# Sums of squares of the first four pairs taken by TensorE from the transposed rows, and an order of work planned with other durations

## The chip, the cores and the metric

The kernel runs on one core of one Trainium2 chip. The metric is the time of one execution on the device in microseconds. The median of three runs before the change is 1098.53 us (1098.04 to 1100.46).

## What is computed

A random-feature attention over 8 batches and 8 heads, followed by an MLP on its output.

```python
batch, n_heads, seq, head_dim = (8, 8, 576, 64)     # n_features m = 128
def phi(x):
    proj = np.einsum('bhsd,md->bhsm', x, omega)
    sq = np.sum(x * x, axis=-1, keepdims=True) / 2.0
    h = proj - sq
    h = h - np.max(h, axis=-1, keepdims=True)
    return np.exp(h) / np.sqrt(m)
q_p, k_p = (phi(q * scale), phi(k * scale))
kv = np.einsum('bhsm,bhsd->bhmd', k_p, v)
z = np.sum(k_p, axis=2)
num = np.einsum('bhsm,bhmd->bhsd', q_p, kv)
den = np.einsum('bhsm,bhm->bhs', q_p, z)[..., None] + 1e-06
attn = num / den
x = attn.transpose(0, 2, 1, 3).reshape(B * S, H * D)    # 4608 x 512
h = x @ w_in                                            # 512 x 2048
out = (h / (1.0 + np.exp(-h))) @ w_out                  # 2048 x 512
```

## The kernel before

Two heads make a pair: 32 pairs, n = 0 to 31, four to a batch. The 2 x 576 rows of a pair are nine blocks of 128 rows; the fifth (MID) holds the last 64 rows of the one head and the first 64 of the other. Each pair's queries and keys come in twice: `raw` (128 x 704, features on partitions, both heads above each other, and at the end a block of 128 columns for the mixed rows) and `nat` (128 x 9 x 64, rows on partitions).

For each pair and for k and q: `project` (L256) multiplies raw with omega on TensorE into two banks of PSUM, `project_mid` (L268) does the mixed block into a third; `square` (L248) squares nat in place on ACT, `square_sum` (L252) sums each row on DVE into `sq`; `top` (L272) takes the row maxima on DVE; `shift` (L280) makes the bias from maximum and sum of squares; `expo` (L294) takes the exponentials on ACT (from pair 8 on `lower` and `expo_all` do this in another way). Then `sums` (L314) adds the key features on POOL, `zsum` (L325) finishes that on TensorE and `zcopy` copies it; `kv`, `kt_copy`, `kv_turn` and `kw_copy` make the 128 x 64 matrices; `products`, `denom` (DVE) and `normal` (L372, POOL) normalise the queries; `turn` (L377) transposes them in three groups g = 0, 1, 2, `en_copy` copies these, and `numer` (L394) makes x, which `x_high` and `x_low` split into two float32r parts.

The MLP goes through nine column tiles of 512 tokens, t = 0 to 8, and in each through sixteen steps f of 128 hidden columns: `stage1` (s1, L489: for each k of the four pairs of a batch three matmuls), `silu` on ACT, `g_low` on DVE, and `stage2` (s2, L507) two steps later. So s1(0, f, k) needs x of pair k, and the first tile needs pairs 0 to 3. The weights arrive as 64-bit words; ACT (`exponent`), DVE (`word`, three operations) and POOL (`weight_high`, `weight_low`) make two float32r parts of each. w_out's are written to memory and read again for each tile.

The order of all this isn't written out. `Plan` (L64) holds units of work, each with an engine, an assumed duration, a key (a due time from `at` and `clock`), what it must follow (`after` for data, `order` for sequence alone) and the ring buffers and PSUM banks that it takes and frees. `Plan.run` simulates the engines and emits the units one by one; the framework then places the single instructions into each engine's queue, which runs in order, and may interleave those of neighbouring units. Pairs 0 to 3 (`LEAD = 4`, "calm" in the code) form the start, due every 11 us; the later pairs are due along the steps of the MLP. Pairs below 8 (`DIRECT`) take their exponentials from PSUM. nat has two buffers.

Of the kernel before, what the change touches and what calls it, by code (L numbers as in the profile page):

```python
# [197 lines left out]
def attention_mlp(ctx: ExitStack, tc: tile.TileContext, qT, kT, qn, kn, v, om_in, w_in, w_out, out):  # L198
# [10 lines left out]
    def new(tag, shape, dtype=F32):  # L209
        return ring.tile(shape, dtype, tag=tag, name=tag, bufs=RINGS[tag])  # L210
# [6 lines left out]
    oms = const.tile([P, M], F32, tag="oms", name="oms")  # L217
    prod = const.tile([P, NC, M + 1], F32, tag="prod", name="prod")
# [21 lines left out]
    def load_nat(n, who):  # L240
        T["nat", n, who] = nat = new("nat", [P, NC, D])
        nc.sync.dma_start(nat, (kn if who == "k" else qn)[divmod(n, NPAIR)])
# [5 lines left out]
    def square(n, who):  # L248
        nat = T["nat", n, who]
        nc.scalar.activation(nat, nat, AF.Square, scale=SCALE * 0.5**0.5)  # L250
# [17 lines left out]
    def project_mid(n, who, ps):  # L268
        nc.tensor.matmul(ps[:, :M], T.pop(("raw", n, who))[:, S:], oms, start=True, stop=True)  # L269
        T["p", n, who, 2] = ps  # L270
# [277 lines left out]
    for n in range(NWIN):  # L548
        calm = n < LEAD
        for i, who in enumerate("kq"):  # L550
# [3 lines left out]
            def prev(s):  # L554
                return [(s,) + x for x in last]
# [3 lines left out]
            before = [("nat", n, "k")] if i else ([("nat", n - 1, "q")] if n else [])  # L559
            add(("nat",) + w, "SP", 0.42, at(n, i - 13.5, 8.1 + 10 * i - 32), lambda n=n, who=who: load_nat(n, who),  # L560
                order=before, alloc=[("nat", ("nat",) + w)], lat=1.1)
            add(("sq",) + w, "ACT", 0.7, at(n, 2 * i - 4, 13 + 10 * i - 32), lambda n=n, who=who: square(n, who),
                after=[("nat",) + w])
            add(("ssum",) + w, "DVE", 0.78, at(n, 2 * i - 3, 14 + 10 * i - 32), lambda n=n, who=who: square_sum(n, who),
                after=[("sq",) + w], order=prev("ssum"), alloc=[(f"sq{who}", ("ss",) + w)], free=[("nat",) + w])
# [3 lines left out]
                after=[("raw",) + w, "omega"], order=prev("proj"),  # L569
# [3 lines left out]
            add(md, "PE", 0.25, at(n, 3 * i + 0.1, o + 5.2), lambda ps, n=n, who=who: project_mid(n, who, ps),  # L573
                banks=1, after=mid_after, free=[("raw",) + w])
# [5 lines left out]
            if calm:  # L580
                add(("nb", n, who, 0), "DVE", 0.45, at(n, 3 * i + 1.5, 0), lambda n=n, who=who: shift(n, who, every),
                    after=[("top", n, who, j) for j in range(3)] + [("ssum",) + w], free=[("ss",) + w])
            else:
                add(("nb", n, who, 0), "DVE", 0.5, at(n, 0, o + 1.4), lambda n=n, who=who: shift(n, who, sides),
                    after=[("top", n, who, j) for j in range(2)] + [("ssum",) + w])
                add(("nb", n, who, 2), "DVE", 0.4, at(n, 0, o + 5.8), lambda n=n, who=who: shift(n, who, middle),
                    after=[("top", n, who, 2), ("ssum",) + w], free=[("ss",) + w])
            for j in range(3):
                b = bk(md) if j == 2 else bk(pj, j)
                nb = ("nb", n, who, 0 if calm else j & 2)  # L590
                if n < DIRECT:
                    add(("exp", n, who, j), "ACT", 0.4 if j == 2 else 1.15,
                        at(n, 3 * i + 2 + 0.1 * j, o + 1.6 + (4.4 if j == 2 else 0.1 * j)),
                        lambda n=n, who=who, j=j: expo(n, who, j), after=[nb], table="exp", free=[b])
                else:
                    add(("low", n, who, j), "DVE", 0.36 if j == 2 else 0.7,
                        at(n, 0, o + 1.5 + (4.4 if j == 2 else 0.1 * j)),
                        lambda n=n, who=who, j=j: lower(n, who, j), after=[nb], free=[b])
# [9 lines left out]
        add(("sums", n), "POOL", 3.2, at(n, 6, 25), lambda n=n: sums(n), after=e["k"], order=[("sums", n - 1)] if n else [],  # L608
# [16 lines left out]
        add(("prod", n), "DVE", 1.7, at(n, 8, 34.2), lambda n=n: products(n),  # L625
# [4 lines left out]
        for g in range(3):  # L630
            add(("norm", n, g), "POOL", 0.85, at(n, 9 + 0.1 * g, 37 + 0.1 * g), lambda n=n, g=g: normal(n, g),
# [27 lines left out]
    def weight(i, key, src, last, more=()):  # L659
# [4 lines left out]
        for s in range(3):  # L664
            add(("wd",) + i + (s,), "DVE", (0.5, 0.78, 0.75)[s], key - 2 + 0.1 * s, lambda s=s: word(i, s),
                after=([("wd",) + i + (s - 1,), ("re",) + i] if s else [("wl",) + i]),
                order=[("wd",) + last + (0,)] if last and not s else [],
                alloc=[] if s else [("w32", ("w32",) + i)],
                free=([("wraw",) + i] if s == 2 else [("wre",) + i] if s == 1 else []))
        add(("wh",) + i, "POOL", 0.9, key - 1, lambda: weight_high(i), after=[("wd",) + i + (2,)], alloc=list(more))  # L670
        add(("wlo",) + i, "POOL", 1.05, key, lambda: weight_low(i), after=[("wh",) + i], free=[("w32",) + i])
# [102 lines left out]
```

## Time and profile before

| | us |
|---|---|
| median of three runs | 1098.53 |
| the profiled execution | 1101.4 |
| its span, first to last instruction | 1099.3 |
| TensorE busy in the span | 1053.1 |
| DVE, ACT, POOL busy | 566.4, 583.1, 255.5 |
| mean granted TensorE clock | 0.976 |

The profile is of one execution. A line of a group names the line of the kernel, the engine, the operation, the output and inputs by the program's names, their shape and the count, the busy time and the mean of one in ns, and then the time that the engine was idle just before and who ended that. A line of the timeline begins with its start and its length in us; neighbouring instructions of one kind are merged, and their count stands behind the x. A fp32 matmul appears as two records, its two passes. In the chain that ended last each row has start, length and what ran.

### The profile page before, as it was taken

To read this page: it belongs to the slowest core of one execution; us is meant where nothing else is said; L and a number is where in the kernel's file an instruction comes from. 1 tells how busy PE (TensorE), PEld (TensorE's weight loads), DVE (VectorE), ACT (ScalarE), POOL (GpSimd) and SP (SyncE) were. 2 spreads that over 40 slices of the span, in tenths; PEclk is the share of its full clock that TensorE was granted. 3 is DMA by queue.
4 is the path that set the end of the run, shared out by engine and by line. 5 is a ranking of instruction groups with operands and counts; after the bars stand their busy time and mean duration, and the time that the engine had idled before them with its cause. 6 is when DMAs were issued, how large, how long until landed. Compare 5 with 4: busy or idle time off the path is not lost.

```text
span 1099.3 us, 16192 instructions
## 1 busy us (share of the span) xinstructions
PE 1053.1 (96%) x5900; PEld 834.5 (76%) x5900; DVE 566.4 (52%) x1109; ACT 583.1 (53%) x1085; POOL 255.5 (23%) x327
## 2 busy tenths in 40 slices
PE   5677998899999999999999999999999999999998
PEld 4455776687877778777778777787877788888886
DVE  6788897745555455545555455555554431111111
ACT  5557878565556555555556555655565442222211
POOL 3666665411111111111111111111111110000000
PEclk7688999999999999999999999999999999999999
DMA  7576787553335443444345433533343226223323
GB/s 282 198 221 234 265 290 252 182 167 125 124 126 178 139 133 119 136 165 138 122 139 178 140 127 130 173 131 126 123 154 104 80 80 213 96 96 122 109 96 96
DMA packets 66526, 167.84 MB, mean 153 GB/s; under 512 B 15632, under 2 KB 15760, under 8 KB 66448
## 3 DMA queue, kind: packets, MB, share of 16 engines
q1 hardware_dynamic: 65984, 166.23, 45.6%
q8 instruction: 47, 0.77, 0.3%
q10 hardware_dynamic: 464, 0.59, 0.1%
q14 instruction: 31, 0.25, 0.1%
HBM read 146.87 MB, written 19.92 MB: 152 GB/s over the span
## 4 chain that ended last, share of the span: by engine, by line
PE 86%; DVE 5%; DMA 3%; ACT 3%; POOL 1%; issue 1%; SPq 0%; ACTq 0%; DVEq 0%; POOLq 0%
PE ps_acc L513 35%; PE ps_h L495 34%; PE ps_att L262 5%; PE ps_att L343 3%; PE ps_att L381 3%; PE ps_att L399 2%; DMA wraw<-w_out 1%; DMA nat<-qn 1%; PE ps_att L327 1%; PE ps_att L269 1%; DVE w L458 1%; ACT hq L298 1%; DVE w L462 1%; POOL hq L375 1%; DVE den L369 1%
## 5 line engine op out<-in xcount | busy, mean ns | idle before, releaser
L513 PE MATMUL ps_acc<-wo,gh 128*128 128x512 f32 x1152 | 369.9, 402 | 0.0
L500 ACT ACTIVATE gh<-ps_h 128x512 fp32r<-128x512 f32 x144 | 86.2, 599 | 295.9 <-PE ps_h L495 295.3
L505 DVE TENSOR_TENSOR gl<-ps_h,gh 128x512 fp32r<-128x512 f32 x144 | 99.1, 688 | 275.8 <-ACT ps_h L501 275.8
L513 PEld LDWEIGHTS ps_acc<-wo,gh 128*128 128x128 f32 x1152 | 207.1, 189 | 43.7
L495 PE MATMUL ps_h<-xh,wh 128*128 128x512 f32 x576 | 235.0, 409 | 0.3 <-ACT xh L413 0.3
L495 PE MATMUL ps_h<-xh,wl 128*128 128x512 f32 x576 | 226.7, 394 | 0.0
L495 PE MATMUL ps_h<-xl,wh 128*128 128x512 f32 x576 | 225.9, 392 | 0.0
L513 PE MATMUL ps_acc<-wo,gl 128*128 128x512 f32 x576 | 225.8, 392 | 0.0
L375 POOL TENSOR_TENSOR hq<-hq,rd 128x384 f32<-128x384 f32 x96 | 81.7, 879 | 421.4 <-DVE rd L370 396.5
L495 PEld LDWEIGHTS ps_h<-xh,wh 128*128 128x128 f32 x576 | 108.1, 188 | 24.7 <-issue 0.8
L513 PEld LDWEIGHTS ps_acc<-wo,gl 128*128 128x128 f32 x576 | 108.1, 188 | 24.2 <-issue 0.8
L495 PEld LDWEIGHTS ps_h<-xh,wl 128*128 128x128 f32 x576 | 108.1, 188 | 24.1
L495 PEld LDWEIGHTS ps_h<-xl,wh 128*128 128x128 f32 x576 | 108.5, 188 | 22.3 <-DVE xl L418 0.4
L312 ACT ACT_TABLE_LOAD x48 | 61.6, 1283 | 69.2 <-DVE hq L303 53.3
L318 POOL TENSOR_TENSOR t<-hk 128x256 f32<-128x256 f32 x64 | 48.8, 780 | 183.2 <-ACT hk L312 170.1
L278 DVE TENSOR_REDUCE mxq<-ps_att 128x4 f32<-128x512 f32 x57 | 37.2, 687 | 99.7 <-PE ps_att L262 99.6
L501 ACT ACTIVATE ps_h<-ps_h 128x512 f32<-128x512 f32 x144 | 85.3, 593 | 0.0
L500 ACT ACT_TABLE_LOAD x56 | 71.8, 1283 | 22.0 <-PE ps_h L495 21.3
L362 DVE TENSOR_TENSOR prod<-hq,zb 128x512 f32<-128x512 f32 (+1 forms) x96 | 52.3, 595 | 49.6 <-ACT zb L336 47.7
L250 ACT ACTIVATE nat<-nat 128x576 f32<-128x576 f32 x64 | 44.6, 703 | 20.3 <-DMA nat<-kn 12.3
L381 PE MATMUL ps_att<-ident,hq 128*128 128x128 f32 x261 | 41.1, 284 | 7.9 <-POOL wp L476 2.4
L278 DVE TENSOR_REDUCE mxk<-ps_att 128x4 f32<-128x512 f32 x55 | 35.6, 686 | 18.7 <-PE ps_att L262 18.7
(121 smaller groups left out, 1232.0 us busy)
## 6 DMA issues: line engine op xcount, KB each, us to landing
wo<-wo_d SPq DMA_DIRECT2D x144, 512.0 KB, 3.3
rawk<-kT SPq DMA_DIRECT2D x32, 352.0 KB, 3.0
rawq<-qT SPq DMA_DIRECT2D x32, 352.0 KB, 3.8
v<-v SPq DMA_DIRECT2D x32, 320.0 KB, 2.9
nat<-kn SPq DMA_DIRECT2D x32, 288.0 KB, 3.3
nat<-qn SPq DMA_DIRECT2D x32, 288.0 KB, 3.2
wraw<-w_in SPq DMA_DIRECT2D x16, 512.0 KB, 4.6
wraw<-w_out SPq DMA_DIRECT2D x16, 512.0 KB, 4.3
```

Of the source, the lines that this page charges most:

```text
L262: nc.tensor.matmul(ps[:, i * M : (i + 1) * M], raw[r, o : o + P], oms[r], start=True, stop=True)
L278: nc.vector.tensor_reduce(m[:, 5 * j : 5 * j + 4], ps.rearrange("p (c m) -> p c m", m=M), AX.X, ALU.max)
L312: nc.scalar.activation(h, h, AF.Exp)
L318: nc.gpsimd.tensor_tensor(t[:, j], e[:, 5 * j : 5 * j + 2], e[:, 5 * j + 2 : 5 * j + 4], ALU.add)
L362: nc.vector.tensor_tensor(prod[:, c, :M], e[:, c], zb[:, j].unsqueeze(1).broadcast_to([P, hi - lo, M]), ALU.mult)
L375: nc.gpsimd.tensor_tensor(e[:, c], e[:, c], rd[:, c].unsqueeze(2).broadcast_to([P, 3, M]), ALU.mult)
L381: nc.tensor.transpose(ps[:, i * P : (i + 1) * P], T["h", n, "q"][:, 3 * g + i], ident)
L495: nc.tensor.matmul(ph, w[:, k, :], x, start=k == 0 and n == 0, stop=k == NK - 1 and n == 2)
L500: nc.scalar.activation(gh, ph, AF.Silu)
L501: nc.scalar.activation(ph, ph, AF.Silu)
L505: nc.vector.tensor_tensor(gl, T["ph", t, f], T["gh", t, f].bitcast(F32), ALU.subtract)
L513: nc.tensor.matmul(T["po", t][j], g[:, js], w, start=f == 0 and n == 0, stop=f == NF - 1 and n == 2)
```

## The change

For pairs 0 to 3 nat is no longer loaded and DVE no longer sums rows. ACT squares the transposed rows (raw, 704 columns) into a buffer of the nat ring, now 704 columns wide. TensorE sums them over the 64 features of a head: nine matmuls with the squares as the stationary operand and one moving column, which has ones for the one head (`head`) or for both (the mixed block). They write nine columns beside the result of the middle block, and stand ahead of it; `shift` reads them from PSUM. So `mid` now waits for the squares, and a `proj` of these pairs is ordered behind the `mid` before it. From pair 4 on all is done as before. The plan also gets other durations for several units.

```diff
+    head = const.tile([P, 2], F32, tag="head", name="head")
+    nc.vector.memset(head, 0.0)
+    for j in range(2):
+        nc.vector.memset(head[j * D : (j + 1) * D, j : j + 1], 1.0)
...
     def load_nat(n, who):
-        T["nat", n, who] = nat = new("nat", [P, NC, D])
+        T["nat", n, who] = nat = new("nat", [P, S + P])[:, : NC * D].rearrange("p (c d) -> p c d", d=D)
...
     def square(n, who):
+        if n < LEAD:
+            T["rs", n, who] = rs = new("nat", [P, S + P])
+            nc.scalar.activation(rs, T["raw", n, who], AF.Square, scale=SCALE * 0.5**0.5)
+            return
...
     def project_mid(n, who, ps):
-        nc.tensor.matmul(ps[:, :M], T.pop(("raw", n, who))[:, S:], oms, start=True, stop=True)
+        raw = T.pop(("raw", n, who))
+        if n < LEAD:
+            rs = T.pop(("rs", n, who))
+            T["sq", n, who] = ps[:, M : M + NC]
+            for i in range(4):
+                for j in range(2):
+                    o = REST * j + i * P
+                    c = M + 5 * j + i
+                    nc.tensor.matmul(ps[:, c : c + 1], rs[:, o : o + P], head[:, j : j + 1], start=True, stop=True)
+            nc.tensor.matmul(ps[:, M + MID : M + MID + 1], rs[:, S:], ones[:, :1], start=True, stop=True)
+        nc.tensor.matmul(ps[:, :M], raw[:, S:], oms, start=True, stop=True)
...
+            if calm:
+                add(("sq",) + w, "ACT", 0.78, at(n, 3 * i - 0.5, 0), lambda n=n, who=who: square(n, who),
+                    after=[("raw",) + w], alloc=[("nat", ("nat",) + w)])
+            else:
...
             add(pj, "PE", 1.5, at(n, 3 * i, o), lambda a, b, n=n, who=who: project(n, who, a, b), banks=2,
-                after=[("raw",) + w, "omega"], order=prev("proj"),
+                after=[("raw",) + w, "omega"],
+                order=prev("proj") + ([("mid", n, "k")] if i else [("mid", n - 1, "q")] if n else []) * calm,
...
-            add(md, "PE", 0.25, at(n, 3 * i + 0.1, o + 5.2), lambda ps, n=n, who=who: project_mid(n, who, ps),
-                banks=1, after=mid_after, free=[("raw",) + w])
+            add(md, "PE", 1.6 if calm else 0.25, at(n, 3 * i + 0.1, o + 5.2), lambda ps, n=n, who=who: project_mid(n, who, ps),
+                banks=1, after=mid_after + ([("sq",) + w] if calm else []), free=[("raw",) + w] + ([("nat",) + w] if calm else []))
...
-        add(("sums", n), "POOL", 3.2, at(n, 6, 25), lambda n=n: sums(n), after=e["k"], order=[("sums", n - 1)] if n else [],
+        add(("sums", n), "POOL", 3.7 if n < DIRECT else 3.1, at(n, 6, 25), lambda n=n: sums(n), after=e["k"], order=[("sums", n - 1)] if n else [],
```

The other durations are `exp` 1.25 instead of 1.15, `prod` 2.1 instead of 1.7, `norm` 1.0 instead of 0.85, the three `word` operations 0.7, 0.85, 0.85 instead of 0.5, 0.78, 0.75, `wh` 0.8 instead of 0.9 and `wlo` 1.4 instead of 1.05.

What this does to the queues is seen in the program's order. POOL first, its first work of the attention. L318 to L323 before (L336 to L341 after) are a pair's key sums, L375 (L393) the normalisation of a pair's queries, L476 and L480 (L494 and L498) the two parts of a weight. Before:

```order
L318 TENSOR_TENSOR t<-hk 128x256 x2
L320 TENSOR_TENSOR es<-t 128x256
L323 TENSOR_TENSOR es<-es,hk 64x128 x2
L375 TENSOR_TENSOR hq<-hq,rd 128x384 x3
L476 CAST wh_322<-w_231 128x512
L318 TENSOR_TENSOR t<-hk 128x256
L480 TENSOR_TENSOR wl_323<-w_231,wh_322 128x512
L318 TENSOR_TENSOR t<-hk 128x256
L320 TENSOR_TENSOR es<-t 128x256
L323 TENSOR_TENSOR es<-es,hk 64x128 x2
```

The same place after:

```order
L336 TENSOR_TENSOR t<-hk 128x256 x2
L338 TENSOR_TENSOR es<-t 128x256
L341 TENSOR_TENSOR es<-es,hk 64x128 x2
L336 TENSOR_TENSOR t<-hk 128x256 x2
L338 TENSOR_TENSOR es<-t 128x256
L341 TENSOR_TENSOR es<-es,hk 64x128 x2
L393 TENSOR_TENSOR hq<-hq,rd 128x384 x3
L494 CAST wh_403<-w_260 128x512
L498 TENSOR_TENSOR wl_404<-w_260,wh_403 128x512
```

The sums of pair 1 stood behind the normalisation of pair 0 and interleaved with the first weight; now they stand ahead of both.

TensorE from the transposes of pair 0 to x of pair 0. hq is the queries of pair 0, es the key sums of pair 1, v is read by kv(1), en and kw by num(0), rawk is pair 2's. Before:

```order
L381 MATMUL ps_h_315<-ident_75,hq_156 128x128 x3
L381 MATMUL ps_att_329<-ident_75,hq_156 128x128 x3
L381 MATMUL ps_att_337<-ident_75,hq_156 128x128 x3
L327 MATMUL ps_h_412<-es_360,ones_80 128x256
L343 MATMUL ps_att_345<-hk_186,v_118 64x128 x10
L399 MATMUL ps_acc_370<-en_316,kw_266 64x512 x2
L399 MATMUL ps_att_371<-en_316,kw_266 64x64 x2
```

After, with the same names by role (L399 is the transposes now, L345 the key sums, L417 is num, L285 to L287 the group of the middle block with its squares):

```order
L399 MATMUL ps_acc_398<-ident_75,hq_166 128x128 x3
L399 MATMUL ps_acc_410<-ident_75,hq_166 128x128 x3
L399 MATMUL ps_acc_414<-ident_75,hq_166 128x128 x3
L345 MATMUL ps_acc_419<-es_325,ones_80 128x256
L285 MATMUL ps_acc_426<-head_84,nat_333 128x1 x8
L286 MATMUL ps_acc_426<-ones_80,nat_333 128x1
L287 MATMUL ps_acc_426<-oms_83,rawk_170 128x128
L417 MATMUL ps_h_450<-en_399,kw_292 64x512 x2
L417 MATMUL ps_h_451<-en_399,kw_292 64x64 x2
```

kv(1) has gone from between z(1) and num(0) to a place ahead of the transposes; the group of pair 2's keys has come in between.

ACT around the transposed queries of pair 2. en is their copy (L385 before, L403 after), hk the key exponentials of pairs 3 and 4, nat_604 and nat_739 are the queries of pair 4, nat_611 the keys of pair 5, hq_695 the queries of pair 3. Before:

```order
L442 ACTIVATE wre_639<-wraw_554 128x512
L250 ACTIVATE nat_604<-nat_604 128x576
L250 ACTIVATE nat_611<-nat_611 128x576
L385 COPY en_659<-ps_acc_658 128x384
L298 ACTIVATE hk_593<-ps_acc_583,nbk_595 128x128 x4
L298 ACTIVATE hk_593<-ps_att_584,nbk_595 128x128 x4
L385 COPY en_659<-ps_acc_680 128x384
```

After:

```order
L403 COPY en_773<-ps_acc_783 128x384
L403 COPY en_773<-ps_acc_788 128x384
L316 ACTIVATE hk_651<-ps_att_641,nbk_653 128x128 x4
L316 ACTIVATE hk_651<-ps_acc_642,nbk_653 128x128 x4
L258 ACTIVATE nat_739<-nat_739 128x576
L403 COPY en_773<-ps_att_772 128x384
L316 ACTIVATE hq_695<-ps_att_685,nbq_697 128x128 x4
L316 ACTIVATE hq_695<-ps_h_686,nbq_697 128x128 x4
```

The squares of pair 4's queries and pair 5's keys stood ahead of the first copy and of pair 3's key exponentials; now the first of them stands behind two copies and pair 4's key exponentials, and pair 3's query exponentials follow soon.

More of the change, by code (lines that the diff above doesn't have):

```diff
@@ L558, in attention_mlp @@
                 order=prev("raw"), alloc=[(f"raw{who}", ("raw",) + w)], lat=1.3)
[L559 to L565, printed above, removed]
+            if calm:
+                add(("sq",) + w, "ACT", 0.78, at(n, 3 * i - 0.5, 0), lambda n=n, who=who: square(n, who),
+                    after=[("raw",) + w], alloc=[("nat", ("nat",) + w)])
+            else:
+                before = [("nat", n, "k")] if i else ([("nat", n - 1, "q")] if n > LEAD else [("sq", n - 1, "q")])
+                add(("nat",) + w, "SP", 0.42, at(n, 0, 8.1 + 10 * i - 32), lambda n=n, who=who: load_nat(n, who),
+                    order=before, alloc=[("nat", ("nat",) + w)], lat=1.1)
+                add(("sq",) + w, "ACT", 0.7, at(n, 0, 13 + 10 * i - 32), lambda n=n, who=who: square(n, who),
+                    after=[("nat",) + w])
+                add(("ssum",) + w, "DVE", 0.78, at(n, 0, 14 + 10 * i - 32), lambda n=n, who=who: square_sum(n, who),
+                    after=[("sq",) + w], order=prev("ssum") if n > LEAD else [], alloc=[(f"sq{who}", ("ss",) + w)], free=[("nat",) + w])
             o = 6.2 + 10.8 * i
@@ L581, in attention_mlp @@
                 add(("nb", n, who, 0), "DVE", 0.45, at(n, 3 * i + 1.5, 0), lambda n=n, who=who: shift(n, who, every),
-                    after=[("top", n, who, j) for j in range(3)] + [("ssum",) + w], free=[("ss",) + w])
+                    after=[("top", n, who, j) for j in range(3)])
             else:
@@ L591, in attention_mlp @@
                 if n < DIRECT:
-                    add(("exp", n, who, j), "ACT", 0.4 if j == 2 else 1.15,
+                    add(("exp", n, who, j), "ACT", 0.4 if j == 2 else 1.25,
                         at(n, 3 * i + 2 + 0.1 * j, o + 1.6 + (4.4 if j == 2 else 0.1 * j)),
@@ L624, in attention_mlp @@
             alloc=[("kw", ("kw", n))], free=[bk(("ktt", n))])
-        add(("prod", n), "DVE", 1.7, at(n, 8, 34.2), lambda n=n: products(n),
+        add(("prod", n), "DVE", 2.1, at(n, 8, 34.2), lambda n=n: products(n),
             after=e["q"] + [("zc", n)], order=[("den", n - 1)] if n else [], free=[("zb", n)])
@@ L630, in attention_mlp @@
         for g in range(3):
-            add(("norm", n, g), "POOL", 0.85, at(n, 9 + 0.1 * g, 37 + 0.1 * g), lambda n=n, g=g: normal(n, g),
+            add(("norm", n, g), "POOL", 1.0, at(n, 9 + 0.1 * g, 37 + 0.1 * g), lambda n=n, g=g: normal(n, g),
                 after=[("den", n)], order=[("norm", n, g - 1)] if g else [], free=[("rd", n)])
@@ L664, in weight @@
         for s in range(3):
-            add(("wd",) + i + (s,), "DVE", (0.5, 0.78, 0.75)[s], key - 2 + 0.1 * s, lambda s=s: word(i, s),
+            add(("wd",) + i + (s,), "DVE", (0.7, 0.85, 0.85)[s], key - 2 + 0.1 * s, lambda s=s: word(i, s),
                 after=([("wd",) + i + (s - 1,), ("re",) + i] if s else [("wl",) + i]),
@@ L669, in weight @@
                 free=([("wraw",) + i] if s == 2 else [("wre",) + i] if s == 1 else []))
-        add(("wh",) + i, "POOL", 0.9, key - 1, lambda: weight_high(i), after=[("wd",) + i + (2,)], alloc=list(more))
-        add(("wlo",) + i, "POOL", 1.05, key, lambda: weight_low(i), after=[("wh",) + i], free=[("w32",) + i])
+        add(("wh",) + i, "POOL", 0.8, key - 1, lambda: weight_high(i), after=[("wd",) + i + (2,)], alloc=list(more))
+        add(("wlo",) + i, "POOL", 1.4, key, lambda: weight_low(i), after=[("wh",) + i], free=[("w32",) + i])
     last = None
```

## The prediction

> **What bounds the kernel now.** I read the page first, then busy time by stretch, then TensorE's waits, then the chain that ended last.
>
> ```profile
> span 1099.3 us, 16192 instructions
> 0.00:97.00 97.00, 65.08 (x417) 45.58 (x417) 73.97 (x136) 57.90 (x177) 54.92 (x67) 0.75 0.69 230
> 97.00:221.70 124.70, 115.12 (x625) 87.41 (x625) 103.98 (x177) 97.03 (x180) 72.73 (x74) 0.99 0.72 245
> 221.70:1086.60 864.90, 864.69 (x4825) 695.12 (x4825) 386.03 (x794) 425.55 (x723) 127.89 (x187) 1.00 0.40 132
> ```
>
> The long rows give a stretch and its length, then busy PE, weight load, DVE, ACT and POOL, then the granted clock. From 221.7 us on TensorE is busy 864.69 of 864.90 us, and nothing is to be had. The slack lies before: 97.00 - 65.08 = 31.9 us idle in the start, at a clock of 0.75, and 124.70 - 115.12 = 9.6 us in the first sixteen steps of the MLP. In the changed program every engine has, from about the start of step 16 on, the same instructions in the same order as before. TensorE's first of them (k = 1 of that step) begins at
>
> ```profile
> 221.75 0.39 PE L495 MATMUL ps_h<-xh,wh 128*128 128x512 f32 x1
> ```
>
> So the change is worth what it moves this moment; the 1099.3 - 221.75 = 877.5 us behind it stay. What TensorE waits for in the start (total, times, longest):
>
> ```profile
> PE ps_acc L381 <- POOL hq L375: 6.7, 3, 3.4
> PE ps_h L381 <- POOL hq L375: 6.4, 1, 6.4
> PE ps_h L327 <- POOL es L323: 5.5, 1, 5.5
> ```
>
> It waits for the normalised queries (L375) and for the key sums (L323), not for data of its own. The chain says what stood ahead of them (start, length, what):
>
> ```profile
> 2.13 5.31 DMA nat<-qn
> ...
> 27.19 1.02 POOL wh L476
> ...
> 53.83 4.20 DMA nat<-qn
> ...
> 78.37 5.77 DMA nat<-qn
> ```
>
> Loads of natural rows, and weight work on POOL ahead of pair 1's sums. I therefore follow the start in rounds, from one pair's normalisation to the next, and ask in each what is late next once a wait has gone:
>
> ```profile
> 23.70 3.50 POOL L375 TENSOR_TENSOR hq<-hq,rd 128x384 f32<-128x384 f32 x3 [7.97 <-DVE nbq L282]
> 44.55 2.40 POOL L375 TENSOR_TENSOR hq<-hq,rd 128x384 f32<-128x384 f32 x3 [7.26 <-DVE mxk L276]
> 61.71 2.66 POOL L375 TENSOR_TENSOR hq<-hq,rd 128x384 f32<-128x384 f32 x3 [5.64 <-DVE mxk L276]
> 84.40 3.11 POOL L375 TENSOR_TENSOR hq<-hq,rd 128x384 f32<-128x384 f32 x3 [2.84 <-DVE nbk L282]
> 94.66 0.59 ACT L413 CAST xh<-ps_acc 128x512 fp32r<-128x512 f32 x1
> ```
>
> The last row is xh of pair 3, after which the MLP runs freely.
>
> **The price of the new passes.** Each of eight middle matmuls gets nine more with one moving column, eighteen passes. The trace has none. Nearest rows:
>
> ```profile
> 12.80 2.40 PE L343 MATMUL ps_acc<-hk,v 128*64 128x128 f32 x20 [0.24 <-ACT hk L298]
> 45.43 0.90 PE L381 MATMUL ps_acc<-ident,hq 128*128 128x128 f32 x3 [2.69 <-POOL hq L375]
> 123.37 0.27 PE L351 MATMUL ps_att<-ident,kt 128*128 128x128 f32 x1
> 233.30 0.82 PE L381 MATMUL ps_att<-ident,hq 128*128 128x128 f32 x6
> ```
>
> At full clock a pass with 128 columns on both sides takes (0.82 - 0.27) / 5 = 0.11 us; at half clock, behind a wait, about 0.21 ((0.90 - 0.48) / 2, where 0.48 estimates the lone one at half clock). With 64-column weights it was 2.40 / 20 = 0.12 there, so the weight side is about half. Eighteen passes thus cost 1.0 to 2.0 us at full clock, 1.9 to 3.8 at half. I take 1.6, nearest the rows at full clock since the start gets denser; with the old middle matmul of 0.5 a group is 2.1.
>
> The Trainium skill ("TensorE: Matmul & The Clock Gate", section "LDWEIGHTS (loading the stationary operand)") speaks against the cheap end: a weight load takes time by its columns, however little streams behind it. By its 128 / 1.2 GHz eighteen loads are an estimated 1.9 us, and the two groups counted below would cost 0.6 us more. The 64- and 128-column rows above agree that columns count.
>
> **Round by round.** *To the first normalisation.* Pair 0's exponentials waited for the load of 2.13 and start some 2 us sooner. But DVE's products of pair 0 now stand behind the last maximum of pair 1's queries, and that behind its eighteen passes:
>
> ```profile
> 18.45 0.28 DVE L276 TENSOR_REDUCE mxq<-ps_h 128x1 f32<-128x128 f32 x1
> 18.65 0.68 DVE L458 SCALAR_TENSOR_TENSOR w<-wre,w 128x512 uint32<-128x512 uint32 x1
> 19.25 1.49 DVE L362 TENSOR_TENSOR prod<-hq,zb 128x512 f32<-128x512 f32 x3
> ```
>
> Only the word operation between them has left: about 0.5 us.
>
> *0 to 1.* Pair 1's key exponentials no longer wait for nat, and its sums stand on POOL ahead of the first normalisation, in 7.97 idle us. Before, z(1) ran at 33.65:
>
> ```profile
> 27.25 0.90 PE L381 MATMUL ps_att<-ident,hq 128*128 128x128 f32 x3 [0.33 <-POOL hq L375]
> 33.65 1.22 PE L327 MATMUL ps_h<-es,ones 128*128 128x256 f32 x2 [5.50 <-POOL es L323]
> 54.37 0.68 DVE L418 TENSOR_TENSOR xl<-ps_att,xh 128x512 fp32r<-128x512 f32 x1
> 55.83 1.59 DVE L362 TENSOR_TENSOR prod<-hq,zb 128x512 f32<-128x512 f32 x3
> 58.83 0.76 DVE L254 TENSOR_REDUCE sqq<-nat 128x9 f32<-128x576 f32 x1 [1.41 <-ACT nat L250]
> 59.50 1.35 DVE L369 TENSOR_REDUCE den<-prod 128x9 f32<-128x1161 f32 x1
> ```
>
> Now z(1) waits only for its place behind the transposes, 27.25 + 0.90 = 28.15. Then come z 1.22, group (2,k) 2.1, its maximum 0.28, products 1.59, denominator 1.35, and 1.1 for xl of pair 0 (0.68 and its short rest) with the reciprocal: 35.8 instead of 44.55. Beyond the 0.5 that is 8.2 us, one group paid.
>
> *1 to 2.* The stall at 53.83 holds less than it shows: the products of pair 2 ended at 55.83 + 1.59 = 57.42, so the denominator at 59.50 could come only 2.1 us sooner. What is late next is z(2), behind num(1) and group (3,k), 2.1 us. I count 2.0 for the round, in which that group is hidden behind work that ran before, too.
>
> *2 to 3.* Pair 3's queries were projected last, behind pair 2's transposes, kv(3) and num(2):
>
> ```profile
> 72.37 1.33 PE L262 MATMUL ps_acc<-oms,rawq 64*128 64x128 f32 x14
> 77.47 2.42 ACT L298 ACTIVATE hq<-ps_acc,nbq 128x128 f32<-128x128 f32 x9
> ```
>
> Their exponentials began 77.47 - 61.71 = 15.8 us after the normalisation. In the new order this projection and its group stand ahead of all three. What is left ahead on ACT are three copies of 0.48, pair 4's key exponentials (2.18 for eight, below) and one square of 0.69, behind the first 2.7 us of normalisation and transposes: 7.0 us. That would be 8.8; I take 7.8, since one more square's reduction (0.76) is put ahead of the denominator.
>
> ```profile
> 46.74 2.18 ACT L298 ACTIVATE hk<-ps_acc,nbk 128x128 f32<-128x128 f32 x8
> L385 ACT COPY en<-ps_att 128x384 f32<-128x384 f32 x87 | 39.1, 478 | 9.4 <-PE ps_att L381 8.0
> L250 ACT ACTIVATE nat<-nat 128x576 f32<-128x576 f32 x64 | 44.6, 703 | 20.3 <-DMA nat<-kn 12.3 <-DVE mxk L278 4.1 <-DMA nat<-qn 3.8
> ```
>
> *3 to xh.* 10.26 us before; the same chain in the new order: 0.
>
> Together 0.5 + 8.2 + 2.0 + 7.8 = 18.5 us.
>
> **What is given back.** POOL and DVE stretch each other: the normalisation at 23.70 took 3.50 us beside DVE's word operations, that at 44.55 2.40. With sums, normalisations and words closer together I charge 1.1 twice, 2.2. Four rounds laid end to end without a gap are too good; the new groups of pairs 0, 1 and 3, six of 1.6, lie beside loads, exponentials and other waits of TensorE, and if that cover is thin they stand in the open. I charge 1 us a round, 4.0 (all six in the open: 9.6). The squares on ACT now run over 704 columns instead of 576, 0.70 x 128 / 576 = 0.16 us each, 1.3 in all on an engine with 39 us free: nothing.
>
> In the sixteen steps TensorE has the same work in another mixture. The 9.6 us of waits there may shrink or grow; I bound that by half of them either way, 4.8. POOL enters with one w_out less prepared ahead of pair 4's normalisation (nine weights, ten before), 0.75 + 1.34 = 2.1 us, which I charge.
>
> ```profile
> L480 POOL TENSOR_TENSOR wp<-w,wp 128x512 fp32r<-128x512 f32 x16 | 21.4, 1339 | 1.0
> L476 POOL CAST wp<-w 128x512 fp32r<-128x512 f32 x16 | 12.0, 751 | 12.3 <-DVE w L462 11.6 <-DVE nbk L282 0.6
> ```
>
> Sum: 18.5 - 2.2 - 4.0 - 2.1 = 10.2 us. The profiled execution would go from 1101.4 us (span 1099.3) to 1091.2 (1089.1). Against the median of 1098.53 this is 1088.3, rounded to **1088**.
>
> **Rivals.**
> - *Everything is hidden.* 31.9 us idle on TensorE speak for it, the queues of ACT and DVE against. All 18.5: 1080.
> - *A nat wait comes back.* Pair 4's nat now waits until the group of pair 3 has freed its ring; its query square stands on ACT ahead of pair 3's query exponentials. If it is late by the old 4.20 us, 6.0 us are left: 1092.5. Against it: pair 4's exponentials stand in front. If pair 5's are late as well, by the 5.77 of the chain, 0.2 is left: 1098.3.
> - *DVE becomes the bound of the first 222 us.* It is busy 73.97 + 103.98 = 178 of them. Then only its removed work counts, eight reductions of about 0.75 us, 6.0: 1092.5.
> - *Slower: half clock, groups in the open.* The start has a clock of 0.75, and three passes after a wait took 0.90 us. With all eight groups on the path at 3.8 us, 30.4 us take the place of 2 x 1.6 + 4.0 = 7.2: 1088.3 + 23.2 = 1111.5. It turns slower from (10.2 + 7.2) / 8 = 2.2 us a group.
>
> The page named above (the Trainium skill, section "What's actually happening") halves TensorE's clock after an idle window of about 3.4 us and restores it after a busy one. The 0.90 us behind waits and 0.82 us for six in dense work agree; a denser start would then pay the lower price.
>
> **Chances.** Forecast 0.60, everything hidden 0.10, one nat wait back 0.10, DVE 0.09, both waits back 0.05, half clock 0.06. All but the last two lie between 1080 and 1092.5; with most of the bound of the steps beside them: 1078 to 1096. A measurement here can tell about 0.2%, 2.2 us, from no change: faster 0.89, same 0.05, slower 0.06.
>
> **What would show it.** No nat load in the chain before 50 us; z(1) near 28; normalisations near 23, 37, 54 and 71 us; xh of pair 3 near 81 to 82 instead of 94.66; the common order from about 211.5 instead of 221.75; groups of nine one-column matmuls of 1.0 to 2.0 us. It is wrong if those groups cost over 2.2 us in front of waiters, if ACT again sits idle for nat ahead of pair 3's query exponentials, or if the sixteen steps stretch by what the start gained.

## The result, and the profile after

| | median, us | range |
|---|---|---|
| before | 1099.49 | 1098.04 to 1100.98 |
| after | 1113.18 | 1109.88 to 1113.54 |

The ratio is 1.0118, with a 95% interval of 1.0099 to 1.0136: slower by 1.2%. The forecast was 1088, the range 1078 to 1096. The rival with half the clock and the groups in the open had said 1111.5.

Busy time by stretch in the changed kernel, with the columns as before (stretch, length, PE, weight load, DVE, ACT, POOL, granted clock, DMA share and rate):

```profile
0.00:97.00 97.00, 89.95 (x542) 75.23 (x543) 57.05 (x116) 51.78 (x157) 46.78 (x60) 0.77 0.58 191
97.00:233.30 136.30, 118.89 (x643) 89.81 (x642) 111.13 (x192) 98.55 (x197) 80.19 (x81) 0.94 0.72 236
233.30:1098.00 864.70, 864.70 (x4825) 694.74 (x4824) 385.62 (x792) 425.61 (x723) 127.48 (x187) 1.00 0.41 131
```

The long last stretch is what it was (864.70 us, 864.90 before), as forecast. In the start TensorE is now busy 89.95 of 97.00 us instead of 65.08: it hardly waits any more, the others wait for it (DVE fell from 73.97 to 57.05, POOL from 54.92 to 46.78). In the sixteen steps it stands idle 136.30 - 118.89 = 17.4 us, 9.6 before. The moment from which both kernels have the same order (the first matmul with k = 1 of step 16), from the timeline:

```profile
233.85 0.39 PE L513 MATMUL ps_h<-xh,wh 128*128 128x512 f32 x1
```

That is 12.1 us later than before (221.75), and the span is 12.0 us longer: the whole loss lies ahead of this moment. The chain that ended last, at its head:

```profile
6.67 3.50 PE ps_acc L285 x16
10.17 0.43 PE ps_acc L286 x2
10.60 0.64 PE ps_acc L287 x2
11.23 2.01 PE ps_acc L270 x16
13.24 3.50 PE ps_h L285 x16
...
19.82 3.50 PE ps_att L285 x16
...
24.38 2.33 PE ps_acc L361 x20
```

No load of natural rows is left in it, as forecast. In their place stand the new passes (L285 for the eight matmuls of the heads, L286 for the mixed block), back to back with the projections (L270). The normalisations, and xh of pair 3:

```profile
36.53 3.17 POOL L393 TENSOR_TENSOR hq<-hq,rd 128x384 f32<-128x384 f32 x3 [1.95 <-DVE rd L388]
50.60 2.40 POOL L393 TENSOR_TENSOR hq<-hq,rd 128x384 f32<-128x384 f32 x3 [3.74 <-DVE nbk L301]
72.42 2.40 POOL L393 TENSOR_TENSOR hq<-hq,rd 128x384 f32<-128x384 f32 x3
91.37 2.40 POOL L393 TENSOR_TENSOR hq<-hq,rd 128x384 f32<-128x384 f32 x3 [0.68 <-DVE rd L388]
100.34 0.73 ACT L431 CAST xh<-ps_att 128x512 fp32r<-128x512 f32 x2
```

They were at 23.70, 44.55, 61.71, 84.40 and 94.66. The first comes 12.8 us later; of the rounds behind it three are shorter than before and one is longer, and xh of pair 3 starts 5.7 us late. Two groups in the timeline, the second one and the one of pair 3's keys:

```profile
13.17 3.57 PE L285 MATMUL ps_h<-head,nat 128*128 128x1 f32 x16
16.61 0.57 PE L286 MATMUL ps_h<-ones,nat 128*128 128x1 f32 x2
17.03 0.77 PE L287 MATMUL ps_h<-oms,rawq 128*128 128x128 f32 x2
...
62.81 1.95 PE L285 MATMUL ps_acc<-head,nat 128*128 128x1 f32 x16
64.61 0.36 PE L286 MATMUL ps_acc<-ones,nat 128*128 128x1 f32 x2
64.84 0.49 PE L287 MATMUL ps_acc<-oms,rawk 128*128 128x128 f32 x2
```

From the start of L285 to that of L287 eighteen passes take 3.86 us in the one and 2.03 us in the other, 0.214 and 0.113 a pass. I call these the slow and the full pace. The slow pace holds until about 27 us, though TensorE has no gap there. It then comes back in the midst of dense work, at 31 us, and stays until 61.7, so that groups at 41.93 and 50.46 are slow again:

```profile
4.60:27.00 22.40, 22.40 (x130) 20.72 (x132) 6.56 (x18) 7.98 (x24) 3.08 (x5) 1.00 0.51 175
...
27.60:31.00 3.40, 3.40 (x33) 2.78 (x29) 1.29 (x2) 2.71 (x12) 0.72 (x1) 1.00 0.35 96
31.00:61.70 30.70, 30.43 (x161) 24.95 (x162) 21.22 (x38) 16.93 (x50) 18.97 (x21) 0.50 0.44 135
```

The clock column says 1.00 in the first of these stretches, where the spacing of the passes says half; in the other two it agrees with the spacing.

### The profile page after: what moved, and what is told of

Its sections match the earlier page's. It is cut to its first block, busy times and chain, and to the rows that moved or that the text cites. A ratio compares the mean times of both kernels' runs of the same rounds, so it can differ in the third digit from the quotient of the medians.

```text
span 1111.3 us, 16446 instructions
## 1 busy us (share of the span) xinstructions
PE 1082.3 (97%) x6044; PEld 866.7 (78%) x6044; DVE 556.2 (50%) x1104; ACT 578.5 (52%) x1081; POOL 254.5 (23%) x327
## 4 chain that ended last, share of the span: by engine, by line
PE 88%; DVE 7%; ACT 2%; issue 2%; DMA 1%; POOL 1%; SPq 0%; DVEq 0%; ACTq 0%; POOLq 0%
PE ps_acc L531 35%; PE ps_h L513 34%; PE ps_att L270 6%; PE ps_att L361 3%; PE ps_att L399 3%; PE ps_att L417 2%; DVE w L476 1%; DVE prod L380 1%; PE ps_att L287 1%; PE ps_att L345 1%; PE ps_acc L285 1%; DVE w L480 1%; PE ps_acc L361 1%; ACT hk L316 1%; DVE w L474 1%
## 5 line engine op out<-in xcount | busy, mean ns | idle before, releaser
L393 POOL TENSOR_TENSOR hq<-hq,rd 128x384 f32<-128x384 f32 x96 | 79.9, 860 | 403.4 <-DVE rd L388 397.2
L336 POOL TENSOR_TENSOR t<-hk 128x256 f32<-128x256 f32 x64 | 46.8, 747 | 202.2 <-ACT hk L330 166.2
L380 DVE TENSOR_TENSOR prod<-hq,zb 128x512 f32<-128x512 f32 (+1 forms) x96 | 55.3, 626 | 47.8 <-ACT zb L354 45.0
L399 PE MATMUL ps_att<-ident,hq 128*128 128x128 f32 x258 | 40.5, 284 | 7.6 <-ACT hk L316 4.0
L387 DVE TENSOR_REDUCE den<-prod 128x9 f32<-128x1161 f32 x32 | 43.6, 1362 | 0.8
```

Of the source, the lines that this page charges most:

```text
L336: nc.gpsimd.tensor_tensor(t[:, j], e[:, 5 * j : 5 * j + 2], e[:, 5 * j + 2 : 5 * j + 4], ALU.add)
L380: nc.vector.tensor_tensor(prod[:, c, :M], e[:, c], zb[:, j].unsqueeze(1).broadcast_to([P, hi - lo, M]), ALU.mult)
L393: nc.gpsimd.tensor_tensor(e[:, c], e[:, c], rd[:, c].unsqueeze(2).broadcast_to([P, 3, M]), ALU.mult)
L399: nc.tensor.transpose(ps[:, i * P : (i + 1) * P], T["h", n, "q"][:, 3 * g + i], ident)
```

## The experiments

Theory A: the eighteen passes of each group cost the time. Its rival B: the order that the new durations make. Four runs tell them apart.

**New durations alone, in the kernel before.**

```diff
-                    add(("exp", n, who, j), "ACT", 0.4 if j == 2 else 1.15,
+                    add(("exp", n, who, j), "ACT", 0.4 if j == 2 else 1.25,
...
```

> The kernel before, with the new durations of exp, sums, prod, norm, word, wh and wlo in the plan, and nothing else of the change: natural rows are loaded for all pairs, TensorE gets no new passes. Theory A (the eighteen passes of each group cost the time, the order little): the normalisation of pair 0 stays near 23.7 us and the time within 6 us of the kernel before, 1094 to 1105. Theory B (the order that the new durations make costs it, above all in the sixteen steps): 1108 or more.

1101.54 us, ratio 1.0014 (1.0001 to 1.0026): next to nothing. The first normalisation is at 22.20.

**Squares by TensorE alone, with the old durations.**

```diff
-                    add(("exp", n, who, j), "ACT", 0.4 if j == 2 else 1.25,
+                    add(("exp", n, who, j), "ACT", 0.4 if j == 2 else 1.15,
...
```

> The changed kernel with the old durations in the plan (the middle matmul of pairs 0 to 3 stays at 1.6, the new squares at 0.78), so the squares by TensorE alone. Theory A: the normalisation of pair 0 near 36 us as in the changed kernel, time 1108 to 1118. Theory B: near the kernel before, 1096 to 1103.

1129.21 us, ratio 1.0264 (1.0240 to 1.0287): slower than either theory had it. The first normalisation is at 36.26 as in the changed kernel, so the four groups ahead of it cost what they cost there; the round from pair 2 to pair 3 is the one that breaks, 29.4 us instead of 19.0:

```profile
74.19 2.40 POOL L393 TENSOR_TENSOR hq<-hq,rd 128x384 f32<-128x384 f32 x3 [5.01 <-DVE rd L388]
103.58 2.40 POOL L393 TENSOR_TENSOR hq<-hq,rd 128x384 f32<-128x384 f32 x3 [2.48 <-DVE rd L388]
```

The re-estimated durations thus gain 16 us, but only beside the groups. Why that round breaks wasn't followed further.

**One matmul of nine columns for the nine of one column.**

```diff
-            for i in range(4):
-                for j in range(2):
-                    ...
-            nc.tensor.matmul(ps[:, M + MID : M + MID + 1], rs[:, S:], ones[:, :1], start=True, stop=True)
+            nc.tensor.matmul(ps[:, M : M + NC], rs[:, S:], ones[:, :NC], start=True, stop=True)
```

> The changed kernel with its plan, order and waits, but one matmul with nine moving columns instead of the nine with one: two passes instead of eighteen in each of the eight groups. It leaves out the true sums of squares of pairs 0 to 3 (all nine columns get that of the middle block). Theory A: each group gives back 16 passes, 3.5 us at half clock and 1.9 at full; four of them stand ahead of the first normalisation, which comes near 24 us instead of 36.5, and the time falls by 10 to 18 us to 1095 to 1103. Theory B: the order costs it, the time stays within 4 us of the changed kernel, 1109 to 1117.

1092.74 us, ratio 0.9931 (0.9909 to 0.9952). Same plan, same order, 128 passes fewer: 20.4 us less than the changed kernel, and 2.3 us below the range that A gave. B is out as the cause of the loss. Its normalisations, xh of pair 3 and the start of the common order:

```profile
23.64 3.56 POOL L388 TENSOR_TENSOR hq<-hq,rd 128x384 f32<-128x384 f32 x3 [0.47 <-DVE rd L383]
36.61 2.40 POOL L388 TENSOR_TENSOR hq<-hq,rd 128x384 f32<-128x384 f32 x3 [1.26 <-DVE nbk L296]
53.38 2.40 POOL L388 TENSOR_TENSOR hq<-hq,rd 128x384 f32<-128x384 f32 x3 [1.11 <-DVE rd L383]
71.06 2.40 POOL L388 TENSOR_TENSOR hq<-hq,rd 128x384 f32<-128x384 f32 x3 [0.68 <-DVE rd L383]
79.66 0.72 ACT L426 CAST xh<-ps_att 128x512 fp32r<-128x512 f32 x2
211.64 0.39 PE L508 MATMUL ps_h<-xh,wh 128*128 128x512 f32 x1
```

The prediction said near 23, 37, 54 and 71, 81 to 82, and 211.5. Without the passes the stations of the forecast come out nearly, which is luck in part (see below).

**Every group twice.**

```diff
+            for _ in range(2):
...
```

> The changed kernel with each group of nine one-column matmuls issued twice: 36 passes instead of 18 in each of the eight groups, same result. Theory A: another four times 3.9 us ahead of the first normalisation (near 52 us), and about 2.1 each for the later four as far as they stand on the path: 1128 to 1138. If the groups lie beside other waits of TensorE, as I had forecast for pairs 0, 1 and 3: under 1120.

1139.99 us, ratio 1.0361 (1.0329 to 1.0393): 26.8 us more than the changed kernel for 144 passes, 0.19 each, and 2 us above the range expected. The first normalisation comes at 48.30 instead of 36.53. While such a group runs, nothing else is at work:

```profile
30.00:35.00 5.00, 5.00 (x25) 5.00 (x25) 0.00 (x0) 0.00 (x0) 0.00 (x0) 1.00 0.00 0
```

Five microseconds with TensorE alone at work. A holds. What stays open is the pace: in this run TensorE has no gap for over 30 us and yet keeps the slow one until about 39 us. Theory N says that passes with one moving column don't count as work for the clock; L, that the width is of no account.

**32 equal columns instead of one.**

```diff
-                    c = M + 5 * j + i
-                    nc.tensor.matmul(ps[:, c : c + 1], rs[:, o : o + P], head[:, j : j + 1], start=True, stop=True)
+                    c = M + 32 * (5 * j + i)
+                    nc.tensor.matmul(ps[:, c : c + 32], rs[:, o : o + P], head[:, j], start=True, stop=True)
```

> The changed kernel with 32 equal moving columns in each of the nine matmuls of a group instead of one, same number of passes, same result. In the changed kernel passes follow each other at 0.22 us until 28 us and at 0.12 after, though TensorE has no gap. Theory N (passes with one moving column count as no work for the clock and hold the pace at half): the pace doubles within the first 10 us, the first four groups take 2 us instead of 4, the normalisation of pair 0 comes before 30 us and the time falls to 1098 to 1107. Theory L (the passes cost their weight load, and the slow pace has another cause): within 4 us of the changed kernel, 1109 to 1117, pace as before.

1106.24 us, ratio 1.0063 (1.0044 to 1.0083), but spread from 1100.66 to 1111.71. In the profiled execution, the fastest of these, the pace is full from the first projection on, before any wide pass has run; that part is not the width. (In the changed kernel the pace after 28 us isn't one of 0.12 throughout, as the expectation has it: it falls again at 31.) N's first consequence is borne out, its cause not separated.

**A longer warm-up.**

```diff
-WARM = 6
+WARM = 12
```

> The changed kernel with twelve instead of six matmuls of ones ahead of the first projection, nothing else. If the half pace until 28 us only comes from a warm-up that is too short: first projection about 1.5 us later but at full pace, the first four groups at 2 us, time 1099 to 1107. Theory N: full pace at first, but it falls back to half after the first group or two of one-column passes; the time moves by less than 5 us, 1108 to 1117.

1106.93 us, ratio 1.0063 (1.0035 to 1.0091). The number is what the short warm-up would give, the trace is what N says. Busy time by stretch:

```profile
10.00:12.00 2.00, 2.00 (x16) 2.00 (x14) 1.29 (x2) 2.00 (x9) 0.78 (x2) 0.71 1.02 418
12.00:24.00 12.00, 12.00 (x76) 11.00 (x77) 3.36 (x11) 4.62 (x16) 2.53 (x4) 0.50 0.35 107
```

The first group runs at full pace (1.95 us for sixteen passes), the clock falls to 0.50 during the second, with TensorE busy all the time, and stays there for 12 us.

**Both.** (The edits of the last two runs together.)

> The changed kernel with 32 moving columns in the nine matmuls and with twelve instead of six matmuls of ones at the start: both edits that were run alone. Theory N (one-column passes hold the pace at half, wide ones keep it full): full pace from the first projection until 25 us or later in every execution, time 1098 to 1102 and a smaller spread than with wide columns alone (1100.7 to 1111.7). If width doesn't matter: the pace falls at about 12 us as with twelve matmuls alone, 1104 to 1110.

1098.00 us, ratio 1.0006 (0.9986 to 1.0026). The first three groups in the timeline:

```profile
6.77 1.97 PE L285 MATMUL ps_acc<-head,nat 128*128 128x32 f32 x16
...
10.29 1.97 PE L285 MATMUL ps_h<-head,nat 128*128 128x32 f32 x16
...
13.81 1.97 PE L285 MATMUL ps_att<-head,nat 128*128 128x32 f32 x16
```

The second group, in which the pace fell with one column, keeps it with 32, and so does all that follows until TensorE has waited 1.66 us for pair 0's normalised queries (until 26.95 us); the granted clock falls at 28.7. That is the profiled execution; of the others only the time is known. The time falls by 15.2 us against the changed kernel, with the same number of passes. The smaller spread didn't come: the runs lie in two clusters, 1096.2 to 1098.3 and 1102.2 to 1103.3.

These are single executions, but all kept traces together say the same. In the first 260 us the granted clock falls 13 times although TensorE was never idle in the 3.4 us before: in the changed kernel three times (at 31.01, 65.14 and 71.97 us), with every group twice four times, with the longer warm-up alone three times, with the squares alone twice and with the five matmuls of two columns (below) once. Each time 10 to 30 passes with one or two moving columns stand in those 3.4 us. In the other eleven traces, which have no such groups, a single matmul of nine columns in their place, or 32 or 64 columns, each of 76 falls comes after at least 0.48 us of idle time.

**The warm-up in the kernel before.** (Same edit of WARM.)

> The kernel before with twelve instead of six matmuls of ones at the start: what the longer warm-up is worth by itself. Before, the first projections ran at full pace in the profiled execution and TensorE then waited anyway. I expect no more than 1 us either way, 1098 to 1101. If the warm-up state is what differs from run to run in the start: faster by 2 us or more.

1101.81 us, ratio 1.0018 (1.0000 to 1.0036): it gains nothing there, and lies 0.8 us above the range expected. The warm-up is worth something only in front of the groups.

**One matmul a group with the longer warm-up.** (Both edits shown above.)

> The run with one matmul of nine columns a group (two passes, sums of squares left out in the same way), with twelve matmuls of ones at the start. It is the fourth corner beside the changed kernel (1113.2: eighteen passes, slow pace), the one with wide columns and longer warm-up (1098.0: eighteen, pace kept up at first) and that with one matmul a group (1092.7: two, slow pace until 17 us). If number of passes and pace multiply, so that at the fast pace a pass costs half: 128 passes at 0.06 to 0.08 us lie between it and 1098.0, so 1088 to 1091. If the pace alone cost the time, and passes at full pace are free: 1094 to 1098.

1091.50 us, ratio 0.9929 (0.9907 to 0.9951). With this the table is complete (medians, us):

| | eighteen passes a group | two passes |
|---|---|---|
| six warming matmuls, one column | 1113.18 | 1092.74 |
| twelve; the eighteen with 32 columns | 1098.00 | 1091.50 |

128 passes cost 20.4 us in the upper row, 0.16 each, and 6.5 us in the lower, 0.05 each. Pace and number multiply, and the pace is the larger part. These are shares of the end, not prices of a pass: a slow stretch also slows the work between the groups, and a part of the passes is hidden. The 6.5 is rough, since the lower row has no one pace (in the profiled executions it is full until 28.7 us on the left, until 16.6 on the right) and its left corner has two clusters of times. The kernel before, measured beside each of these runs, had medians of 1098.9 to 1100.0, so a difference of 1 us between two of them says nothing.

**Five matmuls a group.** ACT writes the second head's squares 64 columns further left, so that one matmul serves both heads.

```diff
-                for j in range(2):
-                    ...
+                o, c = i * P, M + 2 * i
+                nc.tensor.matmul(ps[:, c : c + 2], rs[:, o : o + P], head, start=True, stop=True)
```

> The changed kernel with five matmuls in a group instead of nine, same result: ACT writes the squares of the second head 64 columns further left, so that one matmul with two moving columns serves both heads of a block (ten passes instead of eighteen), by three ACT instructions instead of one; the bias of pairs 0 to 3 takes four small DVE operations instead of two. By the run with one matmul a group, 128 passes less were worth 20.4 us, 0.16 us each; 64 passes less then give 10.2: 1103, or up to 1107 if the added ACT and DVE operations stand on the path. If a group's cost isn't in its passes: 1109 or more.

1101.90 us, ratio 1.0033 (1.0013 to 1.0053): 11.3 us for 64 passes less, where 10.2 were expected.

**Five, wide, with the longer warm-up.**

> A version with the same result as the changed kernel and all three cheaper sides: five matmuls a group with 64 moving columns (32 for each head; 32 for the mixed block), squares of the second head moved by ACT, and twelve matmuls of ones at the start. 64 passes less than the version with wide columns and longer warm-up (1098.0) at 0.07 to 0.11 us are 4.5 to 7.0: 1091 to 1094, up to 1096 with the added ACT and DVE operations, so faster than the kernel before. If passes at full pace are free: 1098 or more.

1092.32 us, ratio 0.9922 (0.9895 to 0.9950). This version keeps the changed kernel's computation and is faster than both kernels.

Three runs ask what the start is worth with the squares gone. `shift` subtracts the sum of squares from the maximum and then again from the negated difference, so it cancels but for rounding.

**No squares in pairs 0 to 3.**

```diff
+        if n < LEAD:
+            nc.vector.tensor_scalar(part(T["nb", n, who]), part(T["mx", n, who]), -1.0, None, ALU.mult)
+            return
...
```

> The changed kernel with its plan, without the squares of pairs 0 to 3: neither ACT's squares nor the nine matmuls, and the bias is the negated maximum. It leaves out the sums of squares of these pairs, which shift subtracts and adds again, so that they cancel but for rounding. It is the most that taking away the loads, reductions and squares can give in this order. By 0.16 us a pass it lies 2.6 us below the run with one matmul a group (1092.7): 1087 to 1092. If ACT's squares, too, stood on the path: 1082 to 1087.

1083.56 us, ratio 0.9855 (0.9838 to 0.9871), 9.2 us below one matmul a group, where 2.6 were expected from the passes.

**ACT's squares kept, matmuls gone.** (As the last, with the squares still computed.)

> The changed kernel with ACT's squares of pairs 0 to 3 kept but none of the nine matmuls; the bias is the negated maximum, so the squares are not used (the sums of squares of these pairs are left out, which cancel but for rounding). Against the run with one matmul a group (1092.7) it takes away two passes a group and TensorE's wait for the squares; against the run without squares (1083.6) it adds ACT's squares. If the passes and the wait are the 9 us between those two: 1083 to 1086. If ACT's squares are: 1089 to 1092.

1088.91 us, ratio 0.9910 (0.9888 to 0.9931): about in the middle. So the last two passes, TensorE's wait for the squares and the second operation of the bias are worth some 4 us, ACT's squares up to 5.4. The profiled execution without squares had the full pace from 4.8 us on and this one only from about 13, so a part of those 5.4 may be pace; the two weren't separated.

**No squares for any pair.**

> No sums of squares for any of the 32 pairs: no natural rows are loaded, no squares on ACT, no reductions on DVE, no one-column matmuls, and the bias is the negated row maximum. It leaves out what shift subtracts and adds again, which cancels but for rounding. The plan is made anew with the middle matmul at 0.25. From about 220 us on TensorE sets the time and has the same work, so only the start and the sixteen steps can gain: DVE loses ten reductions of pairs 4 to 8, some 8 us, where it leads the chain. I expect 1074 to 1084, against 1083.6 without the squares of pairs 0 to 3 alone. If the order made anew is worse in the start: up to 1095.

1084.27 us, ratio 0.9867 (0.9848 to 0.9886): no better than without those of the first four pairs, 0.3 us above the range expected. DVE is busy 80.10 of 108 us in its steps, but TensorE still stands idle 9.8:

```profile
97.00:205.00 108.00, 98.20 (x538) 76.07 (x534) 80.10 (x128) 69.72 (x134) 62.28 (x64) 0.95 0.71 229
```

Less work on DVE gained nothing in this order. What holds it up instead wasn't followed.

## Why the prediction was wrong

*The bound.* Right: the loss is the shift of one moment, 12.1 us, and nothing changes behind it.

*The price of the new passes.* This step failed. The bracket was good: 1.0 to 2.0 us at full clock, 1.9 to 3.8 at half, and the groups took 2.03 and 3.86, the upper end of each. The value taken from it, "1.6, nearest the rows at full clock since the start gets denser", was not. Read in the timeline as above, four of the eight groups took 3.86, one 3.70, one 2.27 and two 2.03: 25.5 us in all, against 8 x 1.6 = 12.8.

Two assumptions are in the 1.6. The first was that a pass with next to nothing to stream costs less than the 0.11 us of a full one, by the reading that "the weight side is about half". It doesn't: 0.113 with one moving column, and the same with 32. (By the formula in the Trainium skill, "TensorE: Matmul & The Clock Gate", section "LDWEIGHTS (loading the stationary operand)", eighteen loads are an estimated 1.9 us; the trace agrees at the full pace, with 2.03, and not at the slow one, with 3.86.) The second was that a denser start lifts the clock. It was as dense as can be and slow for 22 us, then slow again from 31 to 61.7. That made a pass 1.9 times as long (0.214 against 0.113), and by the table above most of the loss goes with the pace. (The Trainium skill, on the same page, section "What's actually happening", lets the clock rise after some 3.4 us of sustained work; the 22.40 us of TensorE without a gap at 0.214 us a pass do not bear this out, nor do the 8.18 busy of 8.20 us at the slow pace in the run with ACT's squares alone, which has no such pass.)

*Where the groups stand.* "Beside loads, exponentials and other waits of TensorE", said the prediction of six of them, with 4.0 us for what stands in the open. The cover wasn't there. Three of the four groups of pairs 0 and 1 stand in TensorE's queue ahead of z(0) (L345, at 28.34), which pair 0's normalisation needs; the fourth, at 29.23, holds up the last maximum of pair 1's queries (32.31), and pair 0's products stand behind that on DVE. So the wait for that normalisation, which was to cover them, only moved back. Taking 16 of 18 passes out of each group removes 20.4 us from the end; their time in the changed kernel's trace is about 25.5 x 16 / 18 = 22.7. So little of the added work was hidden. How little isn't known exactly, since other work, too, runs at another pace without the passes.

*The rounds.* Near, but with luck. The run with one matmul a group has 23.64, 36.61, 53.38 and 71.06 against 23, 37, 54 and 71 forecast. But the forecast has 3.2 + 4.0 = 7.2 us of groups in it: without groups its own terms promise 10.2 + 7.2 = 17.4 us. That run, with two passes left of eighteen, gained 7.2 by the medians, so the other terms together were some 9 us too good. With the groups, the first normalisation lost 12.8 us; the round 0 to 1 still gained 6.8 (8.2 forecast, before what was charged back) and 2 to 3 gained 3.7 (7.8), but 1 to 2, forecast 2.0 shorter, became 4.7 longer. The group (3,k) stands in it in the open, ahead of z(2), and (2,q), the group of pair 2's queries, lengthens it in a way that the prediction doesn't have:

```profile
50.46 3.57 PE L285 MATMUL ps_acc<-head,nat 128*128 128x1 f32 x16
53.89 0.56 PE L286 MATMUL ps_acc<-ones,nat 128*128 128x1 f32 x2
...
54.54 0.79 ACT L255 ACTIVATE nat<-rawq 128x704 f32<-128x704 f32 x1 [5.46 <-issue]
...
55.80 2.15 ACT L316 ACTIVATE hk<-ps_att,nbk 128x128 f32<-128x128 f32 x8
```

The nat ring has two buffers. ACT's square of pair 3's queries (54.54) starts when the group of pair 2's queries has read its buffer (53.89 + 0.56 = 54.45), and ACT stands idle 5.46 us ahead of it. Behind it in ACT's queue wait pair 2's key exponentials, whose bias was ready at 50.47. With one matmul a group they start at 36.59, as soon as their bias is there.

The loads of natural rows did leave the chain, and pair 1's sums did move ahead of the first normalisation.

*The squares on ACT.* Put at nothing, "on an engine with 39 us free". Free time on ACT isn't cover for them, as the ring shows above. And with the squares kept and the matmuls gone the time is 1088.91, without either 1083.56: they cost up to 5.4 us, an unknown part of which is pace. The remaining two passes of a group, with TensorE's wait for the squares and the longer bias, are another 3.8.

*The sixteen steps.* Charged with 2.1 us. From xh of pair 3 to the common order it was 221.75 - 94.66 = 127.1 us before, 133.5 after, and 132.0 with one matmul a group, so 5 to 6 us are lost there, and 4.9 of them without the passes. TensorE's longest waits in the steps, in the changed kernel and with one matmul a group:

```profile
PE ps_att L399 <- ACT hk L316: 3.6, 1, 3.6
PE ps_att L287 <- DVE hq L324: 2.8, 1, 2.8
...
PE ps_att L399 <- POOL wl L498: 2.3, 1, 2.3
```

```profile
PE ps_att L394 <- ACT hk L311: 3.6, 1, 3.6
PE ps_att L282 <- DVE hq L319: 2.8, 1, 2.8
PE ps_att L394 <- POOL wl L493: 2.3, 1, 2.3
```

The same waits of the same length: they belong to the order, not to the passes. (Before, the longest were 2.4, 2.0 and 1.4 us.) In that run they were made up for by a start 15.0 us shorter, where 12.3 had been forecast, so that its span came to 1089.0 us, the 1089.1 of the forecast, partly by errors that cancel. (That execution was the fastest of its four; their median is 4.7 us above the forecast of 1088.)

*The rivals.* The one that decided was on the list with a chance of 0.06 and a threshold of 2.2 us a group. The row at hand, 0.90 us for three passes behind a wait, was half clock, and the start's clock was 0.75; the choice between the ends of the bracket was in effect the choice of the sign, and the prediction made it by an argument about the clock that no row carried. That this rival's 1111.5 lies so near is luck in part: it had eight groups of 3.8 us, 30.4 in all, and the trace has 25.5; what it left out (more loss in the steps, ACT's squares, the ring) may account for the rest; no run separates the shares.

## What to carry to other kernels

Price a matmul with few moving columns as a full one: here each of the two fp32 passes took 0.113 us at full pace and 0.214 at the slow one. Take the pace of the stretch where it will run, not that of the dense part. Reductions by TensorE with one moving column are dear for an engine that runs in order: merge them until each stationary operand is loaded once, and look at what waits behind them, on other engines, too, that wait for a buffer which the reduction still reads. Where a bracket's two ends give different signs, look for the row that decides between them before giving the sign a chance.

## What the runs showed of the hardware

- Passes with one or two moving columns go with falls of the granted clock of an engine without gaps: 13 in the five traces that have groups of them, none in the other eleven. In one run it fell from full pace to 0.50 during the second group, while the same passes with 32 columns kept it. What exactly the clock counts isn't settled: with no such pass at all, in the run with ACT's squares alone, the projections still went at the slow pace from 4.6 to about 13 us.
- Whether the pace is full at the first projection (at 4.5 us) differs between executions. With six warming matmuls it was full in the profiled executions of the kernel before, of that with the new durations alone, of that with wide columns, of that without any squares and, from 4.8 us, of that without squares in pairs 0 to 3, and slow in the other six. With twelve it was full in four, and from 7.1 us, in the middle of the first projection (which began at 6.47), in the version with five wide matmuls.
- The clock column reads 1.00 in the first stretch of a trace even where passes are spaced at 0.214 us. Ahead of its first change it can't be relied on.
- Every stretch between two changes of the granted clock is a whole multiple of 3.41 us in all sixteen traces (3.41, 6.83 and 30.72 us in the changed kernel, for instance).
